# Allocating LayerNorm's small tiles ahead of the large buffers in a gated FNet kernel

## Chip, cores and metric

The kernel runs on one core of one Trainium2 chip, in one launch. The metric is the device time in microseconds (us). Before the change three runs took 702.18, 702.39 and 702.93 us; the median is 702.39 us.

## What is computed

The reference takes a 2048 x 512 input x, normalizes its rows, and multiplies an FNet branch (the real part of a two-dimensional Fourier transform, written as products with given matrices) with a gate (a two-layer network with squared ReLU, then SiLU). Cut to what matters:

```
xn = layernorm(x)                                  # rows of 512, no scale or shift
a  = xn @ dft_hid_re.T ;  b = xn @ dft_hid_im.T    # 512 x 512
s  = dft_seq_re @ a - dft_seq_im @ b               # 2048 x 2048
h  = relu(xn @ w1 + b1) ** 2                       # w1: 512 x 1792
g  = silu(h @ w2 + b2)                             # w2: 1792 x 512
return x + s * g
```

## The kernel before, in words

All arithmetic keeps float32 accuracy by splitting every operand into a high part (written by ScalarE, `split_hi`, line 125) and a low part (the rest, written by VectorE, `split_lo`, line 128), both of type float32r. Every product is three matmuls, high x high, high x low and low x high. Most matrix products are also done by a seven-product scheme (Strassen-like), for which VectorE forms sums of blocks. So a prepared operand is a tile of 7 blocks x 2 parts x 256 columns of 4 bytes: 14,336 bytes in each of the 128 partitions. In every such product one operand is loaded into TensorE as weights (128 x 128), the other streams past it as the moving operand (256 columns; 512 in the first stage).

The program is written in the order in which each engine runs it; loads are issued by hand in that order on the SyncE queue. Its stages, with the lines of their matmuls:

1. **First sequence chunks** (L340, 7.7 to 98 us). Row blocks of x are loaded, normalized (`ln_stats`, `ln_root`, `ln_rstd`, `ln_xn`) and split into eight tiles XC[0..7], which stay as weights. The sequence matrices of two chunks of 256 columns stream past, 512 columns to a matmul, from the tiles `ga` and `gb`.
2. **Remaining six chunks** (L325, to 334 us). The same with the seven products: weights XC[j], moving operand `ga` or `gb`, 256 columns, 2,016 matmuls. Results go to DRAM.
3. **Hidden transform** (L705, called by `YUnit`, to about 411 us). Eight units of 84 matmuls. Weights are the operands `yg` in xc2 to xc7; the moving operands are four tiles `wdp0` to `wdp3`, which lie in `wd0`, `wd1`, `xc0` and `xc1`. Each product takes three matmuls with each of the four in turn.
4. **First layer of the gate** (L705, called by `HUnit`, to about 553 us). 28 units of 42 matmuls. Weights are `w1_p`, p = n % 7 for unit n; the moving operands are the tokens `xT`, in xc4 to xc7.
5. **Second layer** (L811, in `outer`, to the end). 28 steps of 42 matmuls. Weights are `g_n` in xc6, xc7 and xc4 in turn (the last one in wd0); the moving operands are `w2_p`, p = n % 7. The results are combined, gated and written out.

In stages 4 and 5 it depends on p in which buffer the operand lies:

```
    W1_HOME = "ga", "gb", "xc2", "xc3", "xc0", "xc1", "wd0"
    W2_HOME = "wd1", "ga", "gb", "xc2", "xc3", "xc0", "xc1"
```

Buffers are allocated from one pool, by tag: the first tile of a tag takes the next free bytes of each partition, as many times as the tag has buffers, and later tiles of the tag take the same place again. So the order in which tags first appear in the code sets all addresses. LayerNorm's working tiles are the tags "bn" (48 bytes in a partition, three buffers) and "sm" (16 bytes, three buffers); with padding to 32 bytes they take 3 x 64 and 3 x 32, together 288 bytes. Before the change they first appear in `ln_stats(0)` and `ln_root(0)` (lines 183 and 192), after most large tiles have got their place and ahead of the last four. The addresses as built, in bytes within a partition:

| tiles (bytes each) | address before | modulo 256 |
|---|---|---|
| constants, biases, statistics | 1,024 to 3,552 | |
| xc0 to xc7 (14,336) | 3,552 to 103,904 | 224 |
| pq00; three buffers "u"; pq01; pq10; pq11 (4,096; 8,192; 4,096 each) | 118,240 to 155,104 | 224 |
| wd1 (16,384) | 159,200 | 224 |
| bn, bn, bn, sm, sm, sm | 175,584 to 175,872 | |
| ga (14,336) | 175,872 | 0 |
| wd0 (16,384) | 190,208 | 0 |
| gb (14,336) | 206,592 | 0 |
| e (8,192) | 220,928 | 0 |

All these sizes, and the offsets of the blocks within the tiles, are multiples of 256 bytes, so a tile's residue is that of every operand read from it.

## Time and profile before

| | |
|---|---|
| median of three runs | 702.39 us |
| the profiled execution, as timed | 701.75 us |
| its span, first to last instruction | 700.0 us |
| TensorE matmul (PE) busy | 693.0 us, 5,440 matmuls |
| TensorE weight load (PEld) busy | 670.1 us |
| VectorE (DVE) busy | 605.6 us |
| ScalarE (ACT) busy | 357.9 us |
| DMA moved | 150.82 MB, 215 GB/s in the mean |

The profile names an instruction by its line, engine and tiles, and gives its start and its length. Matmuls overlap in TensorE's pipeline: a single one with 256 columns is shown some 280 ns long, yet the next starts about 117 to 120 ns after it. So the pace of TensorE isn't the length of a matmul but the distance between starts. It is read from the chain of work that ended last: there, a run of matmuls is one row, with its start, its time in us and its number of matmuls.

### The profile page before, as it was taken

What the parts mean: (1) busy time and instruction counts of PE and PEld (TensorE: products, weight loads), DVE (VectorE), ACT (ScalarE), POOL (GpSimd) and SP (SyncE); (2) the same over time, 40 slices, a digit from 0 to 9 for tenths busy, and PEclk for the clock granted to TensorE, in tenths of its full rate; (3) what the DMA queues carried; (4) which work ended last, traced back from release to release, by engine and by line L of the source; (5) the groups of instructions that cost most, each with busy time, mean ns of one, the idle gap of its engine ahead of it and who ended that gap; (6) DMA issues with size and microseconds to landing.
All of it is one profiled execution on the core that took longest, in us unless ns stands there. A gap on an engine that the chain in (4) does not pass through costs nothing.

```text
span 700.0 us, 13144 instructions
## 1 busy us (share of the span) xinstructions
PE 693.0 (99%) x5440; PEld 670.1 (96%) x5440; DVE 605.6 (87%) x849; ACT 357.9 (51%) x475; POOL 6.4 (1%) x9
## 2 busy tenths in 40 slices
PE   8999999999999999999999999999999999999997
PEld 5778889999999999999999999999999999999997
DVE  7999769999999898788899788899748689989896
ACT  4436544435343343435455358777778764444451
POOL 0000000000000000000000000000000000101000
PEclk9999999999999999999999999999999999999999
DMA  8535756768486754367488457587426956767745
GB/s 298 198 104 197 257 202 219 257 204 290 158 294 211 259 210 166 121 239 274 151 287 280 151 185 287 195 322 266 154 118 197 388 168 188 194 197 195 227 155 157
DMA packets 51723, 150.82 MB, mean 215 GB/s; under 512 B 4944, under 2 KB 19536, under 8 KB 50256
## 3 DMA queue, kind: packets, MB, share of 16 engines
q1 hardware_dynamic: 44096, 129.80, 54.9%
q10 hardware_dynamic: 6208, 18.88, 6.8%
q0 software_dynamic: 1360, 1.31, 1.5%
q8 instruction: 42, 0.69, 0.4%
q14 instruction: 17, 0.14, 0.1%
HBM read 101.98 MB, written 47.99 MB: 214 GB/s over the span
## 4 chain that ended last, share of the span: by engine, by line
PE 94%; DVE 3%; DMA 1%; ACT 1%; issue 1%; SPq 0%; DVEq 0%; ACTq 0%
PE m L325 33%; PE m_o L811 15%; PE r_B L705 13%; PE r_A L705 8%; PE pq_b L340 8%; PE r_C L705 4%; PE r_D L705 4%; PE m_last L811 4%; PE pq_ba L340 2%; PE pq_bc L340 1%; PE pq_bb L340 1%; DMA rows<-rows 1%; DVE yg L128 0%; DMA x<-in_x 0%; DVE bn L185 0%
## 5 line engine op out<-in xcount | busy, mean ns | idle before, releaser
L325 PEld LDWEIGHTS m<-g,xc 128*128 128x128 f32 x2016 | 235.7, 188 | 0.6 <-DVE g L128 0.2
L325 PE MATMUL m<-g,xc 128*128 128x256 f32 x2016 | 236.2, 280 | 0.0
L125 ACT ACTIVATE g<-u 128x1792 fp32r<-128x1792 f32 (+3 forms) x70 | 100.1, 1431 | 143.2 <-PE m L325 47.7
L128 DVE TENSOR_TENSOR g<-u,g 128x1792 fp32r<-128x1792 f32 (+3 forms) x70 | 117.5, 1679 | 23.3 <-ACT g L125 23.1
L811 PE MATMUL m_o<-w,g 128*128 128x256 f32 x882 | 105.7, 282 | 0.0
L811 PEld LDWEIGHTS m_o<-w,g 128*128 128x128 f32 x882 | 105.5, 191 | 0.0
L125 ACT ACTIVATE g<-hr 128x1792 fp32r<-128x1792 f32 (+2 forms) x31 | 47.9, 1556 | 47.2 <-PE m_o L811 25.2
L705 PE MATMUL r_B<-xT,w 128*128 128x256 f32 x504 | 69.4, 282 | 0.0
L340 PE MATMUL pq_b<-g,xc 128*128 128x512 f32 x240 | 66.7, 397 | 1.1 <-ACT xc L125 1.0
L705 PEld LDWEIGHTS r_B<-xT,w 128*128 128x128 f32 x504 | 64.1, 190 | 0.0
L128 DVE TENSOR_TENSOR g<-hr,g 128x1792 fp32r<-128x1792 f32 (+2 forms) x31 | 56.7, 1837 | 7.1 <-ACT g L125 7.1
L340 PEld LDWEIGHTS pq_b<-g,xc 128*128 128x128 f32 x240 | 43.8, 188 | 13.9 <-ACT xc L125 3.1
L705 PE MATMUL r_A<-xT,w 128*128 128x256 f32 x336 | 44.7, 282 | 0.0
L705 PEld LDWEIGHTS r_A<-xT,w 128*128 128x128 f32 x336 | 42.1, 190 | 0.0
L705 PE MATMUL r_B<-wdp,yg 128*128 128x256 f32 x288 | 37.5, 283 | 0.2 <-DVE y L715 0.2
L705 PEld LDWEIGHTS r_B<-wdp,yg 128*128 128x128 f32 x288 | 35.6, 190 | 0.6 <-DVE y L715 0.4
L811 PE MATMUL m_last<-w,g 128*128 128x256 f32 x294 | 35.1, 282 | 0.0
L811 PEld LDWEIGHTS m_last<-w,g 128*128 128x128 f32 x294 | 35.1, 190 | 0.0
L257 DVE TENSOR_TENSOR u<-u 128x512 f32<-128x512 f32 x48 | 32.8, 684 | 1.7 <-DMA u<-in_ct 1.7
L128 DVE TENSOR_TENSOR yg<-yraw,yg 128x1792 fp32r<-128x1792 f32 x13 | 26.2, 2021 | 5.4 <-ACT yg L125 5.4
L306 DVE TENSOR_TENSOR c<-m,c 128x512 f32<-128x512 f32 x42 | 27.2, 684 | 1.7 <-PE m L325 1.0
L125 ACT ACTIVATE yg<-yraw 128x1792 fp32r<-128x1792 f32 x13 | 22.1, 1699 | 7.2 <-DVE yraw L266 5.5
(180 smaller groups left out, 862.7 us busy)
## 6 DMA issues: line engine op xcount, KB each, us to landing
u<-in_ct SPq DMA_DIRECT2D x63, 512.0 KB, 3.7
hd<-h ACTq DMA_DIRECT2D x28, 512.0 KB, 4.8
hr<-hd SPq DMA_DIRECT2D x28, 512.0 KB, 3.9
wdp<-wdd SPq DMA_DIRECT2D x8, 896.0 KB, 7.2
yraw<-pqd SPq DMA_DIRECT2D x13, 512.0 KB, 5.0
pqd<-c SPq DMA_DIRECT2D x6, 1024.0 KB, 4.4
w<-w1d SPq DMA_DIRECT2D x6, 896.0 KB, 8.7
y<-y ACTq DMA_DIRECT2D x8, 512.0 KB, 4.1
```

What stands on the lines that cost most here:

```text
L125: nc.scalar.activation(hi, src, AF.Copy)
L128: nc.vector.tensor_tensor(lo, src, hi.bitcast(F32), op=ALU.subtract)
L257: nc.vector.tensor_tensor(t[:, 0:2], r[:, 0:1].to_broadcast([P, 2, 256]), r[:, 1:3], op=ALU.add)
L306: nc.vector.tensor_tensor(part_(to), m, part_(frm), op=op)
L325: nc.tensor.matmul(ps[:, d], w[:, a_, d * P:(d + 1) * P], halves(mv(b_)), start=first and d == 0 and (a_, b_) == (HI, HI), stop=last and ( ...
L340: nc.tensor.matmul(accs[c][k], w, part[c, j][:, b_, 2 * h:2 * h + 2], start=j == 0 and h == 0 and (a_, b_) == (HI, HI), stop=j == NJ - 1 a ...
L705: nc.tensor.matmul(self.region(REGION[k]), w, mv, start=i == 0 and k in (1, 7), stop=i == len(ops) - 1, skip_group_check=True)
L811: nc.tensor.matmul(m[:, i * 256:(i + 1) * 256], ready[n][:, a_, H_SLOT[a], i * P:(i + 1) * P], W2[p][:, b_, b], start=p == 0 and i == 0 an ...
```

## The change

The first buffers of the two tags are now allocated right behind the statistics, ahead of XC and all other large tiles, and `ln_stats(0)` and `ln_root(0)` take these instead of new ones. The other two buffers of each tag come along with the first.

```
     stats_t = pool.tile([P, 2 * NS], F32, name="stats_t")
+    small = {tag: pool.tile([P, n], F32, tag=tag, bufs=3, name=f"{tag}0_0") for tag, n in (("bn", 12), ("sm", 4))}
     rows = dram.tile([2 * NS, P], F32, name="rows")
...
-        sm = buf("bn", [P, 12], f"bn{j}_{hs.start}")
+        sm = small.pop("bn", None) or buf("bn", [P, 12], f"bn{j}_{hs.start}")
...
-        t = root[j] = buf("sm", [P, 4], f"root{j}_{hs.start}")
+        t = root[j] = small.pop("sm", None) or buf("sm", [P, 4], f"root{j}_{hs.start}")
```

The small tiles move to 3,552 to 3,840. The fifteen large tiles from xc0 to wd1 move up by 288 bytes, so xc0 now lies at 3,840 and wd1 at 159,488; all of them are then at residue 0 modulo 256. ga, wd0, gb and e stay where they are. No instruction is added, removed or reordered on any engine or queue, and no instruction waits for another event than before; only the addresses of operands differ.

## The prediction

> **What bounds the kernel.** I read the busy times first, then the chain of work that ended last.

> ```profile
> PE 693.0 (99%) x5440; PEld 670.1 (96%) x5440; DVE 605.6 (87%) x849; ACT 357.9 (51%) x475; POOL 6.4 (1%) x9
> ...
> PE 94%; DVE 3%; DMA 1%; ACT 1%; issue 1%; SPq 0%; DVEq 0%; ACTq 0%
> ```

> TensorE is busy all the time and carries 94% of the chain; DMA carries 1%. So an address can change the time in two ways: it changes the distance between two matmul starts, of which there are over 5,000, or it slows another engine so much that TensorE begins to wait. The first is read in the chain, in stretches in which nothing but matmuls stands. Each row has start, time and number of matmuls. The first row is from the seven-product chunks, the next two from the second layer:

> ```profile
> 263.93 35.12 PE m L325 x301
> ```
> ```profile
> 595.10 10.02 PE m_o L811 x85
> ```
> ```profile
> 605.00 20.27 PE m_o L811 x169
> ```

> That is 116.7, 117.9 and 119.9 ns from start to start, for the same shape (128 x 128 weights, 256 columns). The second and third are the same line with the same kind of weights, and follow one another. What differs is the home of the moving operand: steps 8 and 9 read w2_1 and w2_2 from ga and gb (residue 0), steps 10 to 13 read w2_3 to w2_6 from xc2, xc3, xc0, xc1 (residue 224). The weights g_n lie at 224 in both.

> The first layer shows the opposite pairing. Its moving operand xT is always at 224. In the first pair of rows the weights w1_6, w1_0 and w1_1 come from wd0, ga and gb (residue 0); in the second pair w1_3 and its neighbours come from xc tiles (224):

> ```profile
> 447.36 1.42 PE r_A L705 x12
> ...
> 457.30 1.43 PE r_A L705 x12
> ...
> 465.86 1.44 PE r_B L705 x12
> ...
> 475.94 1.44 PE r_B L705 x12
> ```

> From 447.36 to 457.30 lie two units, 84 matmuls: 118.3 ns. From 465.86 to 475.94 lie two more: 120.0 ns. So in both stages the pair with both operands at 224 is the slowest, 120 ns, and one aligned operand is worth 1.7 to 2.1 ns. The chunks at L325 (weights XC at 224, moving operand at 0) run at 116.7. In the first stage, with 512 columns,

> ```profile
> 53.26 2.10 PE pq_b L340 x9
> ```

> it is 233.3 ns, just twice 116.7. I read 116.7 ns for 256 columns as the pace of the moving stream itself, and what lies above it as the cost of starting a matmul and its weight load.

> **The change part by part.** The allocation itself adds and removes no instruction, so nothing has a direct cost. The bn and sm tiles move 172 KB down; the instructions that use them are small and the same. What is left is the alignment of fifteen large tiles.

> *TensorE.* After the change every matmul has both operands at 0, a pairing that the trace of before doesn't contain. From below it is bounded by adding both gains: 120.0 - 1.7 - 2.1 = 116.2 ns. From above, as a gain at all, by the better single one, 117.9. I take 116.7, the pace of L325, since twice as many columns take exactly twice as long, and since it lies next to the sum. The chunks and the first stage then gain nothing. The terms of the three later stages come from these rows of the chain:

> ```profile
> 356.38 2.87 PE r_B L705 x24
> ...
> 406.55 2.87 PE r_B L705 x24
> ...
> 430.85 1.44 PE r_B L705 x12
> ...
> 465.86 1.44 PE r_B L705 x12
> ...
> 557.37 103.11 PE m_o L811 x864
> 660.48 27.15 PE m_last L811 x228
> ```

> - Hidden transform: 50.17 us from 356.38 to 406.55 for five units of 84 are 119.45 ns; 672 x 2.77 ns = 1.9 us.
> - First layer: 35.01 us from 430.85 to 465.86 for seven units of 42, one round of all seven w1 tiles, are 119.1 ns; 1,176 x 2.4 ns = 2.8 us.
> - Second layer: 103.11 + 27.15 us for 1,092 matmuls are 119.3 ns, 2.6 above 116.7, so 2.8 us; the 84 others, beside the last of the first layer and in the tail, 0.2 us.

> Together 7.7 us less.

> *What is late next.* The hidden transform starts behind a transfer that TensorE doesn't set:

> ```profile
> 334.28 4.47 DMA rows<-rows
> ...
> 340.49 2.02 DVE yg L128
> ...
> 347.52 1.69 PE r_B L705 x12
> ```

> The chain runs through this DMA, ScalarE and VectorE up to 347.52. What TensorE gains from 334 to there, some 110 matmuls x 2.8 ns = 0.3 us, is waited away. In the second layer TensorE asks VectorE for its operands 2% faster. VectorE is full in a part of it:

> ```profile
> 566.00:576.00 10.00, 9.83 (x13) 1.00 0.28 93
> 576.00:586.00 10.00, 9.79 (x12) 1.00 0.48 147
> 586.00:660.00 74.00, 67.31 (x88) 1.00 0.74 203
> ```

> (stretch, its length, VectorE's busy time.) It is at 98% for 20 us, then at 91%. In those 20 us TensorE gains at most 170 x 3.3 ns = 0.6 us; if VectorE can't follow, that is lost, though a queue of prepared operands can cover it. I take 0.1 of 0 to 0.6.

> *VectorE and ScalarE* themselves. The split reads and writes 1,792 elements between tiles of different or equal residue:

> ```profile
> L128 DVE TENSOR_TENSOR g<-u,g 128x1792 fp32r<-128x1792 f32 x43 | 87.0, 2022 | 17.8 <-ACT g L125 17.7
> ...
> L125 ACT ACTIVATE g<-u 128x1792 fp32r<-128x1792 f32 x43 | 73.5, 1708 | 118.1 <-PE m L325 32.0 <-DVE u L259 20.4 <-issue 20.3
> ...
> L128 DVE TENSOR_TENSOR yg<-yraw,yg 128x1792 fp32r<-128x1792 f32 x13 | 26.2, 2021 | 5.4 <-ACT yg L125 5.4
> ...
> L125 ACT ACTIVATE yg<-yraw 128x1792 fp32r<-128x1792 f32 x13 | 22.1, 1699 | 7.2 <-DVE yraw L266 5.5 <-DVE x0e L259 0.8 <-ACT y L135 0.5
> ```

> g<-u goes from 224 to 0, yg<-yraw from 224 to 224: 2,022 and 2,021 ns, 1,708 and 1,699 ns. Residues don't matter to them; cost nothing.

> *DMA.*

> ```profile
> wdp<-wdd SPq DMA_DIRECT2D x8, 896.0 KB, 7.2
> ...
> w<-w1d SPq DMA_DIRECT2D x6, 896.0 KB, 8.7
> ```

> Of the eight wdp loads six end in tiles at 224, and the median lands after 7.2 us; all six w1 loads of the same size end at residue 0 and take 8.7. Alignment isn't visible there, and with 1% of the chain it could hardly count: I take 0. [...]

> **The sum.** 701.75 - 7.7 + 0.3 + 0.1 = 694.45 us against the profiled execution's own time. The median of the runs shown is 0.64 us above that execution, so I predict 695.1 us for a median.

> **The rivals.**

> *Half the gain.* The 116.7 at L325 may belong to that stage, since in the second layer a moving operand at 0 gave only 117.9 with weights at 224 as well. If 117.9 is all that is to be had, the 3,024 matmuls keep 1.2 ns each, 3.6 us: 698.7 us. Against it: there the weights are aligned too, afterwards.

> *Equal residues collide.* What the 120 ns rows share is not only that both operands are unaligned but that both have the same residue; the faster ones all pair 0 with 224. If the weight load and the moving stream disturb one another when they start at the same phase, 0 with 0 is as bad as 224 with 224, and the change brings that pairing to every matmul. Then the 2,016 at L325 go from 116.7 to 120.0, +6.7 us, and the later stages from 119.45, 119.1 and 119.3 to 120.0, +0.4, +1.1 and +0.8: 711.4 us. It decides as soon as the pace with 0 and 0 is above 118.2 ns, where loss at L325 and gain behind it cancel. For it: the gains of the two one-sided pairings are nearly alike. Against it: a collision of unequal pairs shouldn't exist at all, yet the second layer has 117.9 and the first 118.3 in them, over 116.7; a cost for each unaligned operand gives such steps by itself.

> *Nothing happens.* The pace could follow the place of ga, gb and wd0, which don't move, or their neighbours, rather than their residue; or a loss at L325 could cancel the gain: 702.4 us. For it: L325 and the second layer differ by 1.2 ns at equal residues, so something else than the residue has a part. Against it: the switch from 117.9 to 119.9 ns within one line, and a matching one at other weights in the first layer. [...]

> **How the numbers follow.** Full gain 0.50 (695.1), half gain 0.20 (698.7), nothing 0.12 (702.4), collision 0.18 (711.4). The lower end takes 116.2 ns for all 5,040 matmuls of 256 columns, 5,040 x 0.5 ns = 2.5 us under the forecast: 692.6. The upper end takes in no change: 702.8. Only the collision is left out, 0.18. A measurement of this kernel tells about 0.2% from no change, 1.4 us; faster by more than that 0.70, within 0.12, slower 0.18.

> **What would show it.** In the profile after, the chain's rows at L811 and L705 should show 116.7 ns a matmul (864 in about 101 us), at L325 the same 116.7 as before. The busy means of VectorE and ScalarE at L128 and L125 should stay. Around 347 us a longer wait of TensorE for VectorE's y would be the 0.3 us. I am wrong if L325 slows to 120 ns (collision), if the second layer's steps still alternate with p (nothing to do with residues), or if all settle near 118 (half).

## The result and the profile after

The changed kernel takes **708.95 us** (median of four runs, 708.86 to 709.04) against 702.28 us of the kernel before on the same chip (four runs, 702.02 to 702.93). The ratio is 1.0094, 95% interval [1.0076, 1.0111]: slower by 0.9%. Forecast was 695.1 us, and the time lies above the upper end of the range. The rival that comes nearest is the one called "Equal residues collide" (711.4 us).

The profiled execution took 708.86 us, its span 707.1 us, 7.1 us more than before. In the page after, first the busy times, then the shares of the chain:

```profile
PE 700.9 (99%) x5440; PEld 679.2 (96%) x5440; DVE 606.4 (86%) x849; ACT 357.8 (51%) x475; POOL 6.4 (1%) x9
...
PE 95%; DVE 3%; ACT 1%; issue 1%; DMA 0%; DVEq 0%; ACTq 0%
```

No new wait stands there. TensorE carries even more of the chain, with the same 5,440 matmuls. So the matmuls themselves have drawn apart. The chain shows where. The chunks are one row of it in each kernel; first the row before, then rows after (start, time, what, number of matmuls):

```profile
98.06 232.60 PE m L325 x1986
```
```profile
97.09 242.00 PE m L326 x2016
...
431.23 1.44 PE r_B L706 x12
...
466.51 1.44 PE r_B L706 x12
...
563.71 103.68 PE m_o L812 x864
667.39 27.37 PE m_last L812 x228
```

The chunks go from 117.1 to 120.04 ns a matmul. One round of seven units of the first layer takes 35.28 us for 294 matmuls, 120.0 ns, where 35.01 us stood. The second layer takes 103.68 us for 864 matmuls, exactly 120.0 ns, and 27.37 for 228, again 120.0. There is one pace left for every matmul of 256 columns, in all stages, and it is the slowest that the kernel before had. The page shows the same of the single weight load, whose mean before was 188 ns at L325 and 191 at L811:

```profile
L326 PEld LDWEIGHTS m<-g,xc 128*128 128x128 f32 x2016 | 242.1, 192 | 0.1
...
L812 PEld LDWEIGHTS m_o<-w,g 128*128 128x128 f32 x882 | 106.1, 192 | 0.0
```

The first stage, with 512 columns, went the other way. Its rows in the chain after:

```profile
53.15 2.04 PE pq_b L341 x9
55.19 0.68 PE pq_ba L341 x3
55.87 2.04 PE pq_b L341 x9
```

From 53.15 to 55.87 lie 12 matmuls: 226.7 ns, where 233.3 ns stood.

The 7.1 us by stage: the chunks start at 97.09 in place of 98.06 us, -1.0. They gain 2,016 x 2.92 ns, +5.9. From their end to the row at 563.71 lie 224.6 us in place of 223.2 (the end before worked out as 98.06 + 2,016 x 117.12 ns), +1.4. The two rows of the second layer bring 0.6 and 0.2. Together 7.1.

### The profile page after: what moved, and what is told of

Same layout as the page of the kernel before. It is cut to its first block, busy times and chain, and to the rows that moved or that the text cites. A ratio compares the mean times of both kernels' runs of the same rounds, so it can differ in the third digit from the quotient of the medians.

```text
span 707.1 us, 13144 instructions
## 1 busy us (share of the span) xinstructions
PE 700.9 (99%) x5440; PEld 679.2 (96%) x5440; DVE 606.4 (86%) x849; ACT 357.8 (51%) x475; POOL 6.4 (1%) x9
## 4 chain that ended last, share of the span: by engine, by line
PE 95%; DVE 3%; ACT 1%; issue 1%; DMA 0%; DVEq 0%; ACTq 0%
PE m L326 34%; PE m_o L812 15%; PE r_B L706 13%; PE r_A L706 9%; PE pq_b L341 8%; PE r_C L706 4%; PE r_D L706 4%; PE m_last L812 4%; PE pq_ba L341 2%; PE pq_bb L341 1%; PE pq_bc L341 1%; DMA x<-in_x 0%; DVE bn L186 0%; DVE z L862 0%; ACT yg L125 0%
## 5 line engine op out<-in xcount | busy, mean ns | idle before, releaser
L326 PEld LDWEIGHTS m<-g,xc 128*128 128x128 f32 x2016 | 242.1, 192 | 0.1
L326 PE MATMUL m<-g,xc 128*128 128x256 f32 x2016 | 242.2, 283 | 0.0
L125 ACT ACTIVATE g<-u 128x1792 fp32r<-128x1792 f32 (+3 forms) x70 | 99.8, 1426 | 147.9 <-PE m L326 82.9
L128 DVE TENSOR_TENSOR g<-u,g 128x1792 fp32r<-128x1792 f32 (+3 forms) x70 | 117.6, 1680 | 28.9 <-ACT g L125 28.7
L812 PE MATMUL m_o<-w,g 128*128 128x256 f32 x882 | 106.3, 283 | 0.0
L812 PEld LDWEIGHTS m_o<-w,g 128*128 128x128 f32 x882 | 106.1, 192 | 0.0
L125 ACT ACTIVATE g<-hr 128x1792 fp32r<-128x1792 f32 (+2 forms) x31 | 47.9, 1556 | 47.8 <-PE m_o L812 27.8
L128 DVE TENSOR_TENSOR g<-hr,g 128x1792 fp32r<-128x1792 f32 (+2 forms) x31 | 56.8, 1839 | 7.5 <-ACT g L125 7.4
L812 PE MATMUL m_last<-w,g 128*128 128x256 f32 x294 | 35.4, 283 | 0.0
L812 PEld LDWEIGHTS m_last<-w,g 128*128 128x128 f32 x294 | 35.4, 192 | 0.0
L128 DVE TENSOR_TENSOR yg<-yraw,yg 128x1792 fp32r<-128x1792 f32 x13 | 26.2, 2022 | 5.8 <-ACT yg L125 5.8
L125 ACT ACTIVATE yg<-yraw 128x1792 fp32r<-128x1792 f32 x13 | 22.1, 1698 | 7.1 <-DVE yraw L267 5.3
## 6 DMA issues: line engine op xcount, KB each, us to landing
wdp<-wdd SPq DMA_DIRECT2D x8, 896.0 KB, 6.2
w<-w1d SPq DMA_DIRECT2D x6, 896.0 KB, 9.0
```

The costliest lines, as they stand in the source:

```text
L125: nc.scalar.activation(hi, src, AF.Copy)
L128: nc.vector.tensor_tensor(lo, src, hi.bitcast(F32), op=ALU.subtract)
L326: nc.tensor.matmul(ps[:, d], w[:, a_, d * P:(d + 1) * P], halves(mv(b_)), start=first and d == 0 and (a_, b_) == (HI, HI), stop=last and ( ...
L812: nc.tensor.matmul(m[:, i * 256:(i + 1) * 256], ready[n][:, a_, H_SLOT[a], i * P:(i + 1) * P], W2[p][:, b_, b], start=p == 0 and i == 0 an ...
```

## The experiments

**Theories.** *Collision*: the weight load and the moving stream of TensorE disturb one another when their addresses are equal modulo 256, wherever both lie. *Alignment*: being at a multiple of 256 is itself bad for TensorE or somebody beside it. *Traffic*: now that everything lies at residue 0, TensorE collides with the reads and writes of the other engines or of the DMA. *Place*: the pace follows the buffer, not its residue.

In what follows **d** is the residue of the weights less that of the moving operand, modulo 256. Before, d was 224 at the chunks; after, it is 0 everywhere. All kernels are the changed one with bytes inserted ahead of some tiles, by these lines:

```diff
+    pads = {"ga": 32}
     def buf(tag, shape, name, dtype=F32):
+        if tag in pads:
+            pool.tile([P, pads.pop(tag) // 4], F32, name="pad_" + tag)
```

So four lines are added and, for instance, L326 is L330 there (L331 and L333 in the two kernels that change more lines, which are shown with them). No work is left out in any of them.

### All large tiles at 224, and 32 bytes ahead of ga

The first takes the alignment away and keeps the residues equal. The second gives the chunks the difference of before (d = 224), with XC aligned where before ga was.

```diff
+    pads = {"xc0": 224}      # e2_all224: xc0 to e all at 224
+    pads = {"ga": 32}        # e3_ga32: xc0 to wd1 at 0; ga, wd0, gb, e at 32
```

> 224 unused bytes ahead of xc0: all nineteen large tiles lie at residue 224, none at a multiple of 256, and all are equal to one another. Theory 'equal phase': every matmul of 256 columns starts every 120.0 ns as after the change, and the time is that of the change, 709.0 us within 0.7. Theory 'own alignment': now both operands of every matmul are off, so the time is different from the change's; by the gains that the prediction read, it would be 3 ns a matmul or more away from the aligned case, whichever way, 10 us or more.

> The changed kernel with 32 unused bytes ahead of ga: the fifteen tiles from xc0 to wd1 lie at 0, the four from ga to e at 32. The small tiles stay in front. [...] Theory 'equal phase': the time returns to that of the kernel before, 702.3 us within 1, with 116.7 ns at L326 and 117.9 and 120.0 in turn at L812. Theory 'small tiles' (their new place costs the time): it stays at 709. Theory 'own alignment': the fifteen are aligned and the four are not, a quarter of the tiles off, so a time unlike both.

Measured: **708.93 us** with all at 224, ratio to before 1.0094 [1.0079, 1.0109]; **702.53 us** with the 32 bytes, 0.9999 [0.9989, 1.0008]. The chain of the first:

```profile
97.09 242.03 PE m L330 x2016
...
563.73 103.68 PE m_o L816 x864
```

These are the rows of the changed kernel to 0.03 us, with no large tile at a multiple of 256. Alignment is out: neither good nor bad. *Place* is out too, since with 32 bytes ahead of ga the whole loss is gone; and so is the new place of the small tiles, which this kernel keeps. With the 32 bytes the chunks run, in two windows of the chain:

```profile
222.39 35.69 PE m L330 x303
...
300.99 27.08 PE m L330 x232
```

117.8 and 116.7 ns. The difference of before has two paces here, which change within a stage. So 116.7 was not a fixed price of d = 224.

### Only other engines' operands moved

To tell the collision within TensorE from traffic: all tiles that TensorE reads at 224, and most of the tiles between which only VectorE, ScalarE and DMA work (the sums of the chunks and of the hidden transform, and pq01, pq10 and pq11) at 0, 32 and 64; pq00 and e stay at 224.

```diff
+    pads = {"wd1": 160}
+    def buf_u(name):
+        return buf("u", [P, 8 * CW + 8], name)[:, 8:].rearrange("p (k n) -> p k n", k=8)
-            raw[c, j] = buf("u", [P, 8, CW], f"u{c}_{j}")
+            raw[c, j] = buf_u(f"u{c}_{j}")
-            yraw[n] = buf("u", [P, 8, 256], f"yraw{n}")
+            yraw[n] = buf_u(f"yraw{n}")
```

(The bytes for it come from putting b1 and eps into one small tile.)

> All tiles that TensorE reads (xc0 to xc7, wd1, ga, wd0, gb) are equal, at residue 224; the tiles that only VectorE, ScalarE and the DMAs use are spread: the u views of the chunks at 0, 32 and 64, pq01, pq10 and pq11 at 64. (b1 and eps share a tile to make room.) Theory 'TensorE's own two reads collide' (weight load against moving stream): every matmul of 256 columns starts every 120.0 ns, 709.0 us within 0.7 as after the change. Rival 'engines collide' (TensorE's reads against VectorE's, ScalarE's or the DMAs' traffic in tiles at an equal phase): since that traffic is now off phase, the pace falls to 117 to 118 ns and the time to about 702.

Measured: **708.96 us**, 1.0094 [1.0077, 1.0110]. The chain:

```profile
97.12 238.43 PE m L333 x1986
...
563.74 103.68 PE m_o L819 x864
```

120.06 and 120.0 ns. Moving the sums and their loads away from TensorE's residue changes nothing. The other engines still write into the operand tiles themselves, at 224. What this leaves open the trace of the changed kernel settles: from 406.12 to 407.50 us VectorE, ScalarE and GpSimd do nothing at all, and from 417.5 to 423.9 us the DMA moves nothing; by their starts, the 11 matmuls of the first stretch and the 54 of the second are 120.0 ns apart. *Traffic* falls; the pairing of TensorE's own two operands is what is left.

The run shows one thing more. The bytes put in between (three times 32, and 160) make XC lie an odd multiple of 256 bytes from ga and gb, where the changed kernel has an even one. The chunks run at 120.06 ns there and at 120.04 in the changed kernel, so at d = 0 the odd and the even multiple have one pace.

The two addresses are not independent in the pace: the same matmuls start every 120.0 ns at d = 0 and down to every 113.3 ns at others, as the next runs show.

### A fan of differences

XC[j] is put at residue 32 x j, all else large at 224, so that d takes all multiples of 32. A second fan has steps of 16 bytes.

```diff
+    pads = {f"xc{j}": 32 for j in range(1, 8)}     # e1_fan
```
```diff
+    pads = {"pq00": 96}                            # e7_fan16
-    XC = [buf(f"xc{j}", [P, 7, 2, 256], f"xc{j}", F32R) for j in range(NJ)]
+    XC = [buf(f"xc{j}", [P, 3584 + j % 2 * 4], f"xc{j}", F32R)[:, j % 2 * 4:]
+          .rearrange("p (s a n) -> p s a n", s=7, a=2) for j in range(NJ)]
```

> XC[0] to XC[7] lie at residues 0, 32, 64 ... 224 modulo 256; every other large tile lies at 224. At L325/L326 the weights are XC[j] in turn and the moving operand is always at 224, so the eight tiles show eight phase differences in one run. Theory 'equal phase' (the pace depends on the difference of the two residues): the matmuls with XC[7] (difference 0) start every 120.0 ns. If the period is 256 bytes, the other seven run below 118.5 ns; if it is 128, XC[3] is at 120 too; if it is 64, XC[1], XC[3], XC[5] and XC[7] are at 120 and the other four near 116.7, which makes a mean of 118.3 ns over the 2,016. Theory 'own alignment' (an operand off a multiple of 256 costs something by itself): the moving operand is off everywhere, so all but XC[0] are alike, and slower than XC[0]. Theory 'place' (the tile's position in the partition counts, not its low address bits): all eight run at 120 as in the run after the change.

> XC[0] to XC[7] at residues 0, 16, 32 ... 112, all other large tiles at 224, so d = 32, 48, 64, 80, 96, 112, 128, 144 at L326: the fan again at half the step. Theory 'lines of 32 bytes or more' (the phase counts in units of at least 32 bytes): the 16-byte places in between show the pace of the unit that they lie in, so 48 like 32 or like 64. Theory 'lines of 16 bytes': each step has a pace of its own, and the lowest may lie at 48 or 80 rather than at 64. At 32, 64, 96 and 128 both expect the levels of the first fan: 118.3, 114.2, 119.9, 118.6 ns.

Measured: **701.34 us** with steps of 32, 0.9988 [0.9977, 0.9998]; **700.04 us**, a single run, with steps of 16. Each XC[j] takes 42 matmuls of a chunk. Eight windows of the chain of the first fan, one for each, d = 64, 96, 128, 160, 192, 224, 0, 32 in order:

```profile
142.76 4.77 PE m L330 x42
...
147.53 5.04 PE m L330 x42
...
152.57 4.98 PE m L330 x42
...
157.55 5.04 PE m L330 x42
...
162.59 4.95 PE m L330 x42
...
167.53 4.95 PE m L330 x42
...
172.48 5.04 PE m L330 x42
...
177.52 4.97 PE m L330 x42
```

| d | 0 | 32 | 64 | 96 | 128 | 160 | 192 | 224 |
|---|---|---|---|---|---|---|---|---|
| ns | 120.0 | 118.3 | 113.6 | 120.0 | 118.6 | 120.0 | 117.9 | 117.9 |

The mean of the table is 118.3 ns; the chunks' row of the chain, 1,986 matmuls in 235.15 us, has 118.4. By the starts in the trace the other chunks repeat the table within 0.3 ns, except the first of the six, where a pause falls into d = 96 and d = 64 ran at 117.8. Equal residues are the slowest, as the collision has it, but 96 and 160 are as slow, and the best is 64, below the 116.7 that I took for the floor. It isn't a price for each unaligned operand: here both are unaligned in seven of the eight, with every pace from 113.6 to 120.0. In the second fan, d = 64 and d = 112:

```profile
147.74 4.77 PE m L331 x42
...
162.43 5.15 PE m L331 x43
```

113.6 and 119.8 ns. Steps of 16 bytes count too: d = 80 and 96 lie between, 84 matmuls from 152.51 to 162.43 us, 118.1 ns in the mean and 118.8 and 117.3 by the starts in the trace, while 64 has 113.6 and 117.8 in the two fans. And 96, at 120.0 in the first fan, is at 117.3 in the second, with weights at 64 and moving operand at 224 in both: neither d nor the two residues alone set the pace.

### 192 and 64 bytes ahead of ga

Does the sign of d matter, and is 64 good in a whole stage? 192 bytes ahead of ga make d = 64 at the chunks and in the second layer's steps with w2 in ga or gb, and 192 in the first layer's units with w1 in ga, gb or wd0; 64 bytes make d = 192 and 64.

```diff
+    pads = {"ga": 192}       # e4_ga192
+    pads = {"ga": 64}        # e5_ga64
```

> The changed kernel with 192 unused bytes ahead of ga: xc0 to wd1 at residue 0, ga, wd0, gb and e at 192. The fan showed the pace by the difference d = weights minus moving operand (modulo 256): 120.0 ns at 0, 113.4 to 114.2 at 64, 117.8 at 192. Theory 'phase with direction' (the pace is a function of d alone): L326 has d = 64 throughout and runs at 113.6 ns, the steps of the second layer with p = 1, 2 too; units of the first layer with p = 0, 1, 6 have d = 192, 117.8; all else 120. Sum over the three shapes of 256 columns 587.6 us against 596 before, so about 694 us, if VectorE still keeps up. Rival 'only equality counts' (any unequal pair is as good as any other, and 114 belonged to one tile's neighbours): 117 to 118 ns at L326 and 702 us.

> The mirror of the run with 192: 64 unused bytes ahead of ga. Now d = 192 at L326 and in the second layer with p = 1, 2, and d = 64 in the first layer with p = 0, 1, 6. Theory 'phase with direction': 117.8 ns at L326, 113.6 in those units of the first layer, 117.8 in those steps of the second; sum 596 us, time about 702. Rival 'distance without direction' (64 apart is 64 apart): L326 at 113.6 as in the run with 192, 694 us.

Measured: **696.20 us** for 192, 0.9898 [0.9884, 0.9913]; **703.11 us** for 64, 1.0004 [0.9994, 1.0015]. Four windows of the chain for 192, all within the chunks, at one d:

```profile
109.93 22.11 PE m L330 x195
...
143.89 78.01 PE m L330 x662
...
262.00 37.81 PE m L330 x321
...
300.95 27.09 PE m L330 x239
```

113.4, 117.8, 117.8 and 113.3 ns. The same instructions have two paces, and the change comes near the borders of chunks. One border is seen in the chain of this kernel, where TensorE waited for VectorE's low part:

```profile
249.99 1.83 PE m L330 x16
251.81 2.01 DVE g L128
...
257.74 1.94 DVE g L128
259.68 0.04 issue
259.73 2.39 PE m L330 x18
```

Ahead of it 258 matmuls from 222.46 us on took 29.35 us, 113.8 ns in the mean; behind it the pace was 117.8. For 64 bytes nearly the whole stage ran at the slower one:

```profile
143.97 77.91 PE m L330 x661
```

117.9 ns. Its first 84 matmuls, by their starts in the trace, ran at 113.3; the 9.50 us from 97.40 on hold 85 matmuls, the 37.00 us from 144.00 on 316. So both signs have both paces, and a theory that the sign alone decides falls; that its time for this run, about 702 us, was met is in part luck. As far as these runs go, d sets which paces there are, at the border shown the change from one to the other came where TensorE waited, and at d = 0 there is only the one of 120.0.

### Good differences in more stages

First, XC allocated in the order 2 to 7, 0, 1 with 192 bytes ahead of xc0, which puts three quarters of the chunks and five sevenths of both layers at 64 or 192, and the rest at 0. Then four groups 64 bytes apart, so that no pair of 256 columns has d = 0:

```diff
+    pads = {"xc0": 192}                            # e6_best
-    XC = [buf(f"xc{j}", [P, 7, 2, 256], f"xc{j}", F32R) for j in range(NJ)]
+    XC = {j: buf(f"xc{j}", [P, 7, 2, 256], f"xc{j}", F32R) for j in (2, 3, 4, 5, 6, 7, 0, 1)}
```
```diff
+    pads = {"xc0": 64, "xc4": 64, "pq00": 64}      # e9_all64
-    XC = [buf(f"xc{j}", [P, 7, 2, 256], f"xc{j}", F32R) for j in range(NJ)]
+    XC = {j: buf(f"xc{j}", [P, 7, 2, 256], f"xc{j}", F32R) for j in (2, 3, 0, 1, 4, 5, 6, 7)}
```

> XC tiles allocated in the order 2 to 7, 0, 1, and 192 unused bytes ahead of xc0: xc2 to xc7 at residue 0, all other large tiles at 192. By d alone: L326 has d = 64 for six of eight tiles and 0 for two (mean 115.2 ns), the hidden transform 64 throughout (113.6), the first layer 192 for five of seven p and 0 for two (118.4), the second layer 64 for five of seven and 0 for two (115.4). Theory 'phase with direction': sum 583.6 us, 12 to 13 us under the kernel before, 690 us, or up to 3 more where VectorE (94% busy in the first half of L325 before) becomes the bound. Rival 'only equality counts': 702 within 3.

> Residues for which no pair of weights and moving operand is equal: xc2, xc3 at 0; xc0, xc1 at 64; xc4 to xc7 at 128; wd1, ga, wd0, gb at 192. d is 64 or 192 for most pairs and 128 for a quarter of L326, two sevenths of the first layer (p = 2, 3) and of the second. So far ±64 ran at one of two paces, 113.3 or 117.8 ns, which changed only at a stall of TensorE or a change of partner, and 128 at 118.5. Theory 'phase': nothing at 120.0 any more; between 594 us for the three shapes if ±64 is always at 117.8 (about 700 us) and 577 if it is always at 113.3 (685 us or what VectorE allows); in the middle 693. Rival 'the gain of the runs with 192 was bound to their place': no better than 702.

Measured: **695.95 us**, 0.9898 [0.9881, 0.9914], and **691.53 us** (691.28 to 691.83), 0.9845 [0.9831, 0.9860]. The first missed its 690 because the six tiles at d = 64 stayed on the slower pace, 117.8 ns, through all chunks. A window of its chunks, and its second layer:

```profile
181.92 38.20 PE m L330 x323
...
555.62 99.61 PE m_o L816 x864
```

118.3 and 115.3 ns. In the second kernel, the page's group of the chunks and the second layer in the chain:

```profile
L330 PE MATMUL m<-g,xc 128*128 128x256 f32 x2016 | 232.7, 278 | 0.6 <-DVE g L128 0.3
...
550.39 100.43 PE m_o L816 x864
```

232.7 us busy at the chunks where the changed kernel had 242.2, and 116.2 ns in the second layer. Nothing but addresses differs from the changed kernel, and it is faster than both kernels: 17.4 us under the changed one by the medians, 10.8 under the one before.

## Why the prediction was wrong

- **What bounds the kernel**: right. TensorE carries 95% of the chain, and only the distance between starts moved.
- **The reading of the rows**, where it failed. The step is "I read 116.7 ns for 256 columns as the pace of the moving stream itself, and what lies above it as the cost of starting a matmul and its weight load", with "one aligned operand is worth 1.7 to 2.1 ns". Every fast row of before paired 0 with 224, every row at 120.0 paired 224 with 224. I charged the slow rows to unaligned operands; the runs charge them to equal ones: 120.0 ns with all at 224, 120.0 with all at 0, and 113.6 with both unaligned and 64 apart. Even the steps between the fast rows come out of d: the chunks and the fast steps of the second layer had d = 224, which has 116.7 and 117.8 in the run with 32 bytes ahead of ga, and the fast units of the first layer had d = 32, at 118.3 in the fan. Nor was 116.7 the stream's own pace, as 113.3 shows. The support from 512 columns at twice that time holds at d = 224 alone: at d = 0 226.7 stands beside 120.0, at d = 64 233.3 beside 113.3 and 117.8.
- **TensorE, "I take 116.7"**: the sum of two gains was made for a pairing that the trace didn't contain. It gave 120.0. The -7.7 us became +1.4 in the hidden transform and the first layer and +0.8 in the second, and the chunks, which were to gain nothing, cost 5.9. The first stage, also put at nothing, gained 1.0.
- **What is late next**: the 0.3 and 0.1 us had nothing to be lost from. The chunks end later than before, and the transfer of rows has left the chain (DMA 0%).
- **VectorE and ScalarE at 0**: right. In the changed kernel, where source and target are at 0:

```profile
L128 DVE TENSOR_TENSOR g<-u,g 128x1792 fp32r<-128x1792 f32 x43 | 87.1, 2024 | 24.1 <-ACT g L125 23.9
...
L125 ACT ACTIVATE g<-u 128x1792 fp32r<-128x1792 f32 x43 | 73.3, 1705 | 124.6 <-PE m L326 66.5 <-issue 30.6 <-DVE u L259 9.9
```

  2,024 and 1,705 ns, against 2,022 and 1,708 before.
- **DMA at 0**: right. The issues after, and then those with all tiles at 224:

```profile
u<-in_ct SPq DMA_DIRECT2D x63, 512.0 KB, 3.6
...
wdp<-wdd SPq DMA_DIRECT2D x8, 896.0 KB, 6.2
...
w<-w1d SPq DMA_DIRECT2D x6, 896.0 KB, 9.0
```
```profile
u<-in_ct SPq DMA_DIRECT2D x63, 512.0 KB, 3.7
...
wdp<-wdd SPq DMA_DIRECT2D x8, 896.0 KB, 6.2
...
w<-w1d SPq DMA_DIRECT2D x6, 896.0 KB, 8.7
```

  At most 0.3 us lies between residue 0 and 224 in these rows, in both directions, and none of it on the chain.
- **Nothing happens**: out. 32 bytes ahead of ga gave back the whole 0.9%, 702.53 us against 708.95.
- **Half the gain**: its reason was partly true, since 116.7 at the chunks wasn't to be had everywhere at its d. Its time wasn't.
- **The collision**: right in charging equal residues and in where it decides, since the chunks' pace, above 118.2 ns, turned the sign; L325 at 120 ns is the sign that the prediction named for it. Its picture of a disturbance at equal phase alone falls short, since 96 and 160 reached 120.0 as well. It was 2.4 us too high. The chunks' mean before was 117.1 with their pauses in it, not 116.7, so they lost 5.9 and not 6.7. The first stage gained 1.0. The other 0.5 is the median's distance from the profiled execution, 0.64 us before and 0.1 us after. I held it unlikely because unequal pairs had more than one pace (116.7, 117.9, 118.3). The runs show that they do have several, at one and the same d.

Open is the cause within TensorE. The runs show a dependence on d in steps of 16 bytes, a slowest pace at d = 0 (120.0 ns), and two paces at 64 and 192 (113.3 and 117.8 ns) and at 224 (116.7 and 117.8), which at the border shown changed where TensorE waited. They don't show what in the load and the stream waits for what, why 64 and 192 can reach 113.3 ns, or what picks the pace after such a wait. Whether the paces at other d are the same at odd and even multiples of 256 bytes, as the one at d = 0 is, no run tests by itself.

## What to carry to other kernels

Where TensorE carries the chain, as here with 95%, in matmuls of 256 columns each with a weight load of its own, the addresses of its two operands are worth a look: giving all tiles the same residue was the worst of the choices tried here (708.95 and 708.93 us), groups 64 bytes apart the best (691.53 us). When two one-sided changes each gain alike, test "unequal is good" as hard as "each is good" before adding them up. And a pairing that the trace doesn't contain deserves a chance on the slow side as large as that on the fast side.

## What was not expected of the hardware

```profile
53.39 2.10 PE pq_b L345 x9
56.19 2.10 PE pq_b L345 x9
```

  12 matmuls in 2.80 us, 233.3 again.
- The same instructions at the same addresses run at 113.3 or 117.8 ns for whole chunks. The kernels with d = 0 throughout hold one pace, and their runs lie closer together: 708.86 to 709.17 us in three kernels, where the one with 192 bytes ahead of ga spreads from 694.31 to 696.41.
